# More groups in seven half products, a twelve-operation norm, and multiplies moved from GpSimd to VectorE in a fused attention and gated-MLP kernel

## The chip, the cores and the metric

The kernel runs on one core of a Trainium2 chip. Its engines are named as in the profile: PE is TensorE's matrix unit (PEld its weight loads), DVE is VectorE, ACT is ScalarE, POOL is GpSimd, and SP is SyncE, which here only starts transfers. The metric is the device time of one execution in microseconds (us), as the median of several runs.

## The reference

Inputs are q, k and v, each 8 batches × 8 heads × 576 rows × 64, a gain `g_norm` of 64, and four weight matrices: `w_gate` and `w_val` (512×1536), `w_out` (1536×512) and `w_res` (512×512). Everything is float32 in and out. Cut to what matters:

```python
kv  = einsum('bhsd,bhse->bhde', k, v)
o   = einsum('bhsd,bhde->bhse', q, kv)
o   = o / sqrt(mean(o*o, axis=-1) + 1e-6) * g_norm      # per head
x   = o.transpose(0, 2, 1, 3).reshape(4608, 512)
ffn = (gelu(x @ w_gate) * (x @ w_val)) @ w_out
out = x + sigmoid(x @ w_res) * ffn
```

So a linear attention without softmax, with a root-mean-square norm over each head, gives x. A gated MLP follows, and a sigmoid gate weighs its result before x is added back.

## The kernel before

**Blocks.** A batch gives 576 rows: 512 of them form one block, and the 64 left over of all eight batches together form a ninth block. Blocks 0 to 7 belong to batches 0 to 7; block 8 holds the remainders. While the MLP of block m runs on PE, the attention of batch m + 2 is prepared beside it.

**Slots.** The order of all instructions is written out by hand. Each block has sixteen slots. Slots 0 to 11 are the gate and value products of the twelve hidden slices f of 128; slots 12 to 15 are the two halves of the `w_res` product, then the out projection. Work of other engines is attached to a slot with `at(blk, slot, ...)`, to a point within the out projection with `aside_out`, and to a word within a group of products with `at_word`. An engine executes what it is given in that order, each instruction waiting for what it needs.

**A direct slice** (`m_gval`, L386) is four PE matmuls of 128×512 for the gate and four for the value; ACT applies GELU to the gate (L374) and DVE multiplies it with the value (L375) into `hid`.

**A group in half products** (`gv_group`) does four slices at once. Gate and value are each a 2×2 block product, done with seven half-size products in place of eight, in the manner of Strassen and Winograd. A product is four matmuls of 128×256. This needs four sums of quadrants of x (`token_sums`, once per block, in `ts`) and four of the weights (`weight_sums`, once per group and matrix, in `ws`), which DVE forms in fp16. The order of a group is one line of words (L762):

```python
"1g 1v Eg 5g Ev 5v dg 6g dv 6v Fg 2g Fv 2v 7g g11 7v cg 3g cv 3v h11 g22 4g g12 h12 4v g21 h22 h21"
```

A digit is a product of gate or value. E and d are copies on ACT, F and c additions on DVE that read PSUM, g11 to g22 the GELUs and h11 to h21 the hidden products, of which h22 runs on POOL and the others on DVE. The PSUM tiles are called A, E, F: products 1, 4, 6 and 7 go to A, 2 to E (which starts as a copy of A), 3 and 5 to F.

`GROUPS` (L1151) says which fours of slices are done so: groups 1 and 2 (f 4 to 11) in blocks 2 to 6, all three in blocks 7 and 8. Blocks 0 and 1 have only direct slices. `banks_of` assigns the eight PSUM banks: four serve the MLP (`pmoe`), four the attention (`pattn`), and a block with groups uses banks of both.

**The out projection** (`out_by_products`, L479) is done in seven half products too, with sums over `hid` in `hid_s` (`s_begin`, `s_rest`, `s_last`) and over `w_out` (`wo_sums`). Its results pass PSUM tiles w A, D, E, F; DVE multiplies them with the sigmoid gate into `osb` (L518), POOL adds x (`fin`, L522), and SP stores. In block 0 the projection goes slice by slice instead (`out_by_f`). In block 1 the fins were placed in the first four slots of block 2.

**Attention of a batch.** POOL issues seven loads (`load_batch`), behind a tiny copy `hold` that waits for an earlier transfer (`load_behind`). ACT squares the attention output and DVE reduces it per head (L254). `a_norm` forms the reciprocal root from these sums by a bit-level first guess and three steps; on POOL it takes fifteen operations (L300 to L312). `a_t` (L332, DVE) scales the attention output from PSUM into t; the PSUM bank is free when it has read it. `a_x` (L346) multiplies a row of t by g, and SP transposes the result into xT (`d_xT`). t times g is x itself, which `fin` adds at the end; for blocks 0 and 1 xT is made from t on PE and ACT (`a_xT`), so `a_x` is needed there only before the fins.

## Time and profile before

| | |
|---|---|
| median of 7 runs | 329.94 us (328.15 to 331.95) |
| profiled execution, own time | 330.35 us |
| its span | 328.5 us |
| mean granted PE clock | 0.995 |
| starts of block 1, 2, 3 on PE | 55.69, 92.93, 128.34 us |
| starts of block 4, 5, 6 | 161.88, 195.42, 229.22 us |
| starts of block 7, 8 | 260.98, 291.94 us |

The span is the time from the first to the last instruction of the profiled execution; its own time is 1.85 us longer. In timeline lines the columns are: start in us, duration in us, engine, line, operation, what is written and read (buffer names), and how many instructions follow each other without a gap (the duration is of all of them). In brackets stands the idle time before and what ended it. A line of waits reads: the waiting engine, buffer and line, what it waited for, the total in us, the count and the longest.

### The profile page before, as it was taken

What the parts mean: (1) busy time and instruction counts of PE and PEld (TensorE: products, weight loads), DVE (VectorE), ACT (ScalarE), POOL (GpSimd) and SP (SyncE); (2) the same over time, 40 slices, a digit from 0 to 9 for tenths busy, and PEclk for the clock granted to TensorE, in tenths of its full rate; (3) what the DMA queues carried; (4) which work ended last, traced back from release to release, by engine and by line L of the source; (5) the groups of instructions that cost most, each with busy time, mean ns of one, the idle gap of its engine ahead of it and who ended that gap; (6) DMA issues with size and microseconds to landing.
All of it is one profiled execution on the core that took longest, in us unless ns stands there. A gap on an engine that the chain in (4) does not pass through costs nothing.

```text
span 328.5 us, 7155 instructions
## 1 busy us (share of the span) xinstructions
PE 318.1 (97%) x2816; PEld 224.6 (68%) x2816; DVE 259.3 (79%) x463; ACT 191.2 (58%) x347; POOL 147.8 (45%) x225
## 2 busy tenths in 40 slices
PE   8899999999988999999999999999999999999993
PEld 3544455444846867686768686868587888788882
DVE  6757769679699788888887888697889877687754
ACT  3773485366626683768376846674465466636660
POOL 3792141573794378328731974115511331051232
PEclk9999999999999999999999999999999999999998
DMA  7999999699993689487937693800340030011004
GB/s 248 322 195 204 194 204 173 163 190 124 162 133 96 164 109 116 162 128 91 138 144 145 74 152 130 161 2 3 129 82 0 6 124 2 0 67 66 0 3 128
DMA packets 76692, 38.87 MB, mean 118 GB/s; under 512 B 42098, under 2 KB 74354, under 8 KB 76658
## 3 DMA queue, kind: packets, MB, share of 16 engines
q0 software_dynamic: 38752, 17.17, 41.9%
q1 hardware_dynamic: 37328, 20.71, 24.2%
q10 hardware_dynamic: 578, 0.52, 0.5%
q8 instruction: 22, 0.36, 0.4%
q14 instruction: 12, 0.10, 0.1%
HBM read 38.80 MB, written 9.44 MB: 147 GB/s over the span
## 4 chain that ended last, share of the span: by engine, by line
PE 89%; DVE 5%; DMA 2%; issue 1%; SPq 1%; ACT 1%; POOL 0%; DVEq 0%; ACTq 0%
PE wA L479 11%; PE gps L386 10%; PE vps L386 10%; PE rps L406 10%; PE Av L723 8%; PE Ag L723 8%; PE Fv L723 4%; PE Fg L723 4%; PE fps L423 3%; PE wD L479 3%; PE wE L479 3%; PE w L479 2%; PE wF L479 2%; PE Ev L723 2%; PE Eg L723 2%; DMA kf<-in_k_dram 2%
## 5 line engine op out<-in xcount | busy, mean ns | idle before, releaser
L374 ACT ACTIVATE ge<-gps 128x512 f16<-128x512 f32 x44 | 26.1, 597 | 56.1 <-PE gps L386 56.0
L760 POOL TENSOR_TENSOR hid<-ge,c 128x512 f16<-128x512 f16 x16 | 18.6, 1162 | 82.0 <-ACT ge L754 82.0
L723 PEld LDWEIGHTS <-ws 128*128 128x128 f16 x512 | 50.0, 98 | 7.3 <-issue 1.4
L386 PE MATMUL vps<-xT,wv 128*128 128x512 f16 x168 | 43.1, 379 | 0.3 <-DVE osb L518 0.3
L386 PE MATMUL gps<-xT,wg 128*128 128x512 f16 x168 | 43.1, 379 | 0.0
L522 POOL TENSOR_TENSOR osb<-osb,t 128x512 f32<-128x512 f32 x28 | 32.6, 1190 | 22.1 <-DVE osb L518 21.9
L375 DVE TENSOR_TENSOR hid<-ge,vps 128x512 f16<-128x512 f16 x44 | 29.9, 683 | 14.6 <-PE vps L386 12.1
L479 PEld LDWEIGHTS <-hid_s 128*128 128x128 f16 x384 | 37.6, 98 | 4.3
L406 PE MATMUL rps<-wr,xT 128*128 128x512 f16 x144 | 33.4, 380 | 0.0
L479 PEld LDWEIGHTS <-hid 128*128 128x128 f16 x288 | 28.2, 98 | 5.8 <-issue 0.8
L386 PEld LDWEIGHTS <-wv 128*128 128x128 f16 x168 | 16.4, 98 | 20.4 <-issue 0.8
L386 PEld LDWEIGHTS <-wg 128*128 128x128 f16 x168 | 16.3, 98 | 18.2 <-issue 0.2
L415 ACT ACTIVATE th<-rps 128x512 f32<-128x512 f32 x36 | 21.1, 594 | 8.5 <-PE rps L406 8.5
L254 DVE TENSOR_REDUCE ss<-sq 128x8 f32<-128x512 f32 x32 | 20.1, 678 | 7.3 <-ACT sq L249 7.3
L406 PEld LDWEIGHTS <-xT 128*128 128x128 f16 x144 | 13.5, 98 | 14.4
L744 DVE TENSOR_TENSOR Fg<-Ag,d 128x512 f32<-128x512 f32 x16 | 11.2, 700 | 14.8 <-PE Ag L723 12.2
L723 PEld LDWEIGHTS <-wg 128*128 128x128 f16 x192 | 18.5, 98 | 3.3
L479 PE MATMUL wA<-wo_ts,hid_s 128*128 128x256 f16 x168 | 20.6, 273 | 0.0
L723 PEld LDWEIGHTS <-wv 128*128 128x128 f16 x192 | 18.8, 98 | 2.2
L723 PE MATMUL Av<-ts,ws 128*128 128x256 f16 x128 | 19.2, 272 | 1.1 <-ACT Ev L733 1.1
L420 ACT ACTIVATE th<-th 128x512 f32<-128x512 f32 x36 | 20.1, 641 | 0.0
L754 ACT ACTIVATE ge<-c 128x512 f16<-128x512 f32 x16 | 10.1, 630 | 15.7 <-DVE c L744 15.7
(186 smaller groups left out, 704.2 us busy)
## 6 DMA issues: line engine op xcount, KB each, us to landing
out_dram<-osb SPq DMA_DIRECT2D x14, 512.0 KB, 2.6
qraw<-in_q_dram POOLq DMA_DIRECT2D x7, 512.0 KB, 6.7
k<-in_k_dram POOLq DMA_DIRECT2D x7, 512.0 KB, 10.4
v<-in_v_dram POOLq DMA_DIRECT2D x7, 512.0 KB, 11.8
wg<-in_moe_w_gate_dram POOLq DMA_DIRECT2D x2, 512.0 KB, 8.3
wv<-in_moe_w_val_dram POOLq DMA_DIRECT2D x2, 512.0 KB, 8.8
wo<-in_moe_w_out_dram POOLq DMA_DIRECT2D x2, 512.0 KB, 13.6
out_dram<-osb SPq DMA_DIRECT2D x4, 256.0 KB, 4.3
```

What stands on the lines that cost most here:

```text
L254: nc.vector.tensor_reduce(out=out_, in_=sqs.pop((b, i)), op=ALU.add, axis=mybir.AxisListType.X)
L374: nc.scalar.activation(out=ge, in_=gps, func=AF.Gelu)
L375: nc.vector.tensor_tensor(out=hids[blk][:, f, :], in0=ge, in1=vps, op=ALU.mult)
L386: nc.tensor.matmul(ps[:, j0 * P : j1 * P], lhsT=w[:, cc, :], rhs=xT_t[blk][:, j0:j1, cc, :], start=(cc == 0 and j0 == 0), stop=(cc == NP - ...
L406: nc.tensor.matmul(rps, lhsT=xT_t[blk][:, j, cc, :], rhs=wr16[:, cc, :], start=(cc == 0), stop=(cc == NP - 1),)
L415: nc.scalar.activation(out=th, in_=rps, func=AF.Tanh, scale=0.5)
L420: nc.scalar.activation(out=th, in_=th, func=AF.Copy, scale=0.5, bias=0.5)
L479: nc.tensor.matmul(ps[:, e - es[0], :], lhsT=a[:, f, e * P : (e + 1) * P], rhs=b[:, f, :], start=(start and e == es[0] and f == 0), stop=( ...
L522: nc.gpsimd.tensor_tensor(out=res_all[of], in0=res_all[of], in1=t_t[blk][of], op=ALU.add)
L723: nc.tensor.matmul(out_[:, r, :], lhsT=lhsT, rhs=rhs, start=(first and r == 0 and c == 0), stop=(c == 1), skip_group_check=True,)
L744: nc.vector.tensor_tensor(out=dst, in0=ps["A", u], in1=sb["d", u], op=ALU.add)
L760: eng.tensor_tensor(out=dst, in0=ge[q], in1=source(q, "v"), op=ALU.mult)
```

## The change

- **Block 0**: the last four slices (f 8 to 11) become a group of half products (`last_group`). The token sums of block 0 are formed on DVE ahead of its first hidden products. The weight sums of groups 1 and 2 are placed in other slots of block 0, and two of them at a word of the new group.
- **Block 6**: all three groups are in half products, in the order 0, 1, 2. With an odd number of groups the banks change roles. The later parts of batch 7's attention (`a_t`, `a_x` and the transposes) are placed at words of these groups. The weight sums of group 0, formed in block 6 before, are formed in the groups of blocks 2 to 5.
- **The norm on POOL** takes two steps with other constants: twelve operations in place of fifteen.
- **x of block 0** moves from slot 5 of block 0 to slot 15, still on DVE. **x of block 1** moves from POOL (block 2, slots 0 and 1) to DVE, at words of block 2's groups, and the fins and stores of block 1 move with it.
- **Memory**: some tiles share buffers now (`qr`, `qrT`, `wd`, small constants, the `o32` of batch 7), and the sums of group 0's weights have tiles of their own.

```diff
@@ tiles
-            qr_t[b // 2] = qkvp.tile([P, C], FP16, tag="qr", name="qr")
+            qr_t[b // 2] = qkvp.tile([P, C], FP16, tag="qr", bufs=1, name="qr")
-        st[b]["qrT"] = attnp.tile([P, NP, P], FP16, tag="qrT", name="qrT")
+        st[b]["qrT"] = attnp.tile([P, NP, P], FP16, tag="qrT", bufs=1, name="qrT")
-            w["d"] = finp.tile([P, 2, CH], FP32, tag="wd", bufs=1, name="wd")
+            w["d"] = attnp.tile([P, 2, CH], FP32, tag="o32", name="wd")
-                pool, tag = (wpool, f"ws{n}{g}") if g > 0 else (qkvp, "k16")
-                gv_sums[unit] = pool.tile([P, 4, 2, 2, P], FP16, tag=tag, name="ws")
+                gv_sums[unit] = wpool.tile([P, 4, 2, 2, P], FP16, name=f"ws{n}{g}")
@@ a_norm
+        magic = 0x5F1FFFF9 if eng is nc.gpsimd else 0x5F3759DF
+        if eng is nc.gpsimd:
+            for step in range(2):
+                eng.tensor_tensor(out=a, in0=yy, in1=yy, op=ALU.mult)
+                eng.tensor_tensor(out=a, in0=a, in1=m, op=ALU.mult)
+                c = (-0.703952253, 0.703952253 * 2.38924456) if step == 0 else (0.375, -1.25)
+                eng.tensor_scalar(out=mh, in0=a, scalar1=c[0], scalar2=c[1], op0=ALU.mult, op1=ALU.add)
+                if step == 1:
+                    eng.tensor_tensor(out=mh, in0=mh, in1=a, op=ALU.mult)
+                    eng.tensor_scalar(out=mh, in0=mh, scalar1=1.875, scalar2=None, op0=ALU.add)
+                eng.tensor_tensor(out=yy, in0=mh, in1=yy, op=ALU.mult)
+            return
@@ out_by_products
-            at(blk + 1, 0, lambda: fin((0, 0)))
-            at(blk + 1, 1, lambda: fin((0, 1)), lambda: store(0))
-            at(blk + 1, 2, lambda: fin((1, 0)))
-            at(blk + 1, 3, lambda: fin((1, 1)), lambda: store(1))
+            x = [lambda j=j: a_x(blk, j) for j in range(NJ)]
+            at_word(blk + 1, 0, "h21", *x[0:2], lambda: fin((0, 0)), lambda: fin((0, 1)), lambda: store(0))
+            at_word(blk + 1, 1, "Fv", x[2])
+            at_word(blk + 1, 1, "h21", x[3], lambda: fin((1, 0)), lambda: fin((1, 1)), lambda: store(1))
@@ attn_plan_1 (slot 15 of block 0)
+                *[lambda j=j: a_x(0, j) for j in range(NJ)],
-        return plan, [lambda j=j: a_x(b, j, nc.gpsimd) for j in range(NJ)]
+        return plan
@@ groups
-    GROUPS = {blk: (1, 2) for blk in range(2, B - 1)} | {B - 1: (1, 0, 2), B: (0, 1, 2)}
+    GROUPS = {blk: (1, 2) for blk in range(2, B - 2)} | {B - 2: (0, 1, 2), B - 1: (1, 0, 2), B: (0, 1, 2)}
@@ plan_attn_ahead
+        if b == B - 1:
+            t = [lambda j=j: a_t(b, j) for j in range(NJ + 1)]
+            x = [lambda j=j: a_x(b, j) for j in range(NJ + 1)]
+            for i, word, fs in (
+                (0, "1v", t[2:3]),
+                (0, "Fv", t[3:4]),
+                (0, "h21", t[4:5]),
+                (1, "1v", x[0:2]),
+                (1, "Fv", x[2:3]),
+                (2, "1v", [x[3], lambda: d_xT(b, 0, NJ), x[4], lambda: d_xT(b, NJ, NJ + 1)]),
+            ):
+                at_word(m + 1, i, word, *fs)
+            return
@@ weight sums
-    for slot, u in ((6, ("g", 1)), (8, ("v", 1)), (11, ("g", 2)), (13, ("v", 2))):
+    for slot, u in ((2, ("g", 1)), (4, ("g", 2)), (NF - 1, ("v", 1))):
+    at(0, 6, *sums["v", 2][0:2])
+    at_word(0, 0, "Fv", *sums["v", 2][2:4])
-    for i, f in enumerate(late_sums[0:4]):
-        at_word(B - 2, i // 2, ("Fv", "h21")[i % 2], f)
-    at(B - 2, NF + 1, *late_sums[4:8])
+    for i, f in enumerate(late_sums):
+        at_word(2 + i // 2, i % 2, "Fv", f)
@@ banks_of
+            if len(groups) % 2:
+                ga0, ga1, va0, va1, ge_, gf, ve, vf = ga1, ga0, va1, va0, gf, ge_, vf, ve
@@ main loop
-            slots = [first_gval, None]
+            slots = [lambda: first_gval(token_sums(0, nc.vector)), None]
-            slots += [lambda f=f: m_gval(0, f) for f in range(3, NF)]
+            slots += [lambda f=f: m_gval(0, f) for f in range(3, 2 * GF)]
+            def last_group():
+                x, t = pmoe.turn, pattn.turn
+                ends = {}
+                for i, u in enumerate("gv"):
+                    ends.update({(u, "A"): x[i], (u, "E"): x[2 + i], (u, "F"): t[i]})
+                pmoe.turn = x[2:] + x[:2]
+                pattn.turn = t[2:] + t[:2]
+                gv_group(0, 2, ends, amid_gv.get((0, 0), {}))
+            slots += [last_group, None, None, None]
-            plan[5] = [lambda j=j: a_x(0, j) for j in range(NJ)]
-            if blk == 2:
-                plan.setdefault(0, [])[0:0] = rows[0:2]
-                plan.setdefault(1, []).extend(rows[2:4])
```

## The prediction

> **What bounds the kernel now.** I read the page's busy line first, then the chain of work that ended last by engine, then TensorE's waits.

> ```profile
> PE 318.1 (97%) x2816; PEld 224.6 (68%) x2816; DVE 259.3 (79%) x463; ACT 191.2 (58%) x347; POOL 147.8 (45%) x225
> PE 89%; DVE 5%; DMA 2%; issue 1%; SPq 1%; ACT 1%; POOL 0%; DVEq 0%; ACTq 0%
> PE Av L723 <- ACT Ev L733: 1.1, 1, 1.1
> PE wA L479 <- DVE osb L454: 0.7, 1, 0.7
> PE vps L386 <- DVE osb L518: 0.3, 1, 0.3
> ```

> TensorE is busy for 318.1 of 328.5 us and carries 89% of the last chain, so the time falls only by fewer matmul columns or by removing one of its few stalls. The last three lines (wait, total, count, longest) are nearly all of those after the opening, and all stand around the front of block 2. TensorE's timeline gives the price of four hidden slices in either form (block 3):

> ```profile
> 128.34 1.03 PE L386 MATMUL gps<-xT,wg 128*128 128x512 f16 x4
> ...
> 135.25 0.60 PE L723 MATMUL Ag<-xT,wg 128*128 128x256 f16 x4
> ...
> 141.36 0.60 PE L723 MATMUL Ag<-xT,wg 128*128 128x256 f16 x4
> ```

> From the first start to the second, four direct slices take 6.91 us; a group of products takes 141.36 − 135.25 = 6.11 us, 0.437 per product. **A converted group is worth 0.79 us** if nothing waits.

> In block 2 the direct slices take 7.44 (92.93 to 100.37), 0.53 too much, and the first group 7.45 (to 107.82), 1.34 too much. VectorE's and GpSimd's timelines say why:

> ```profile
> 92.42 1.35 DVE L454 TENSOR_TENSOR ts<-xT,ts 128x512 f16<-128x512 f16 x1
> 93.69 1.64 DVE L518 TENSOR_TENSOR osb<-th,osb 128x512 f32<-128x512 f32 x1
> 100.04 2.46 DVE L346 TENSOR_TENSOR t<-t,g 128x512 f16<-128x512 f16 x2
> 228.72 0.42 DVE L454 TENSOR_TENSOR ts<-xT,ts 128x512 f16<-128x512 f16 x1
> 229.06 0.76 DVE L518 TENSOR_TENSOR osb<-th,osb 128x512 f32<-128x512 f32 x1
> 229.74 0.67 DVE L518 TENSOR_TENSOR osb<-th,wA 128x512 f32<-128x512 f32 x1
> 230.36 1.29 DVE L332 TENSOR_TENSOR t<-op,ny 128x512 f16<-128x512 f32 x2
> ```

> ```profile
> 92.34 2.45 POOL L346 TENSOR_TENSOR t<-t,g 128x512 f16<-128x512 f16 x2
> 99.76 2.45 POOL L522 TENSOR_TENSOR osb<-osb,t 128x512 f32<-128x512 f32 x2
> 123.21 0.22 POOL L300 TENSOR_SCALAR nm<-ss 128x40 f32<-128x40 f32 x1 [1.70 <-DVE ss L254]
> 230.06 0.27 POOL L312 TENSOR_TENSOR ny<-na,ny 128x40 f32<-128x40 f32 x1
> 230.29 4.49 POOL L522 TENSOR_TENSOR osb<-osb,t 128x512 f32<-128x512 f32 x4
> ```

> The same sums cost 1.35 and 1.64 at block 2's front, beside GpSimd's two x multiplies, and 0.42 and 0.76 at block 6's, where GpSimd is at its small norm. A pair of x multiplies takes 2.46 beside two fins and 0.75 alone.

> [...] the PSUM-fed rows stay at 0.67 to 0.69 beside the same GpSimd work. [...] the trace has 6.91/32 = 0.216 and 6.11/56 = 0.109.

> **The change part by part**, in us of this profiled execution (span 328.5, own time 330.35; the 1.85 around the span I leave alone).

> *Block 0's last group*: −0.79. Its added VectorE work is four token sums (0.42 each) and rearranged weight sums (about 0.48 per pair of halves). All run in VectorE's gaps except one: the third v2 weight sum stands behind add Fv, whose end in a group is about 3.66 after the group's start; with 0.42 the sum ends at 4.08, while TensorE wants it for 7v at 3.93 and its weight load 0.1 earlier. The wait is about 0.26 (bounds 0 to 0.5, if the sum before it is late too). Net **−0.53**.

> *x of block 1 off GpSimd*: the last token sum falls 1.35 → 0.42, the last residual product 1.64 → 0.75, the x pair 2.46 → 0.75. That is 0.93 + 0.89 + 1.71 us of VectorE time just ahead of the waits for `osb` and for Ev (which waited for VectorE's hidden product of slice 3), so 0.53 + 1.34 = **−1.88** if nothing new comes. The four rows now cost VectorE 4 × 0.37 = 1.5 us behind h21 and Fv, where it waits for TensorE's next sum; if that cover were gone they would cost at most these 1.5. Block 0's four rows stay on VectorE and only move from slot 5 to slot 15, where its out projection asks VectorE for little and their readers, the fins of block 1's first slots, are far off: 0.

> *What block 2 gives back*. GpSimd's order was x, x, fins, h22, h22, hold, the seven loads, norm; it becomes h22, fin, fin, h22, fin, fin, hold, loads, norm. The fins (1.15 each) now run late: the second pair waits for the x row behind group 2's h21 and runs beside the out stage's `hid_s` sums (0.95 each, two SBUF inputs), on which the last subtraction into wF depends; two collisions of up to 0.9 against the slack there leave about **+0.6** (0 to 0.9). Queued behind the fins are hold and seven DMA issues (116.04 to 121.51 on GpSimd's timeline, 5.5 us), and behind these the norm of batch 4. Two fins and the start of the first set the issues some 4.4 to 6.1 later in the block; 1.70 of this is slack (the norm's wait above), and the shorter norm returns 1.07. So the norm ends 1.4 to 3 late. VectorE's a_t of batch 4 waits for it, and hidden products f0 to f3 of block 3 are queued behind a_t; TensorE has 1.05 to 1.3 of slack before it needs the bank or Ev. Stall about **+1.0** (0.35 to 1.6). The loads themselves, 4 to 6 us later, are used a block later and hidden.

> *Norm on GpSimd in twelve operations*, six norms: three operations of about 0.27 plus 0.08 between, so 1.07 less. In the block ends of 3 to 5 the norm is not on the path, since a_t stands behind VectorE's own work: at 230.36, the norm done at 230.33. Gain 0. But the fins follow the norm on GpSimd: the first moves from 230.29 to about 229, onto the last token sum (228.72) and residual product (229.06), which then cost 0.9 more each when hit. In front of direct slices slack takes most of it (0 to 0.8 each): **+0.2** for two boundaries.

> *Block 6 in three groups*: −0.79. In place of direct slices, which use only banks of the out stage, its first products come at once: 1g, 1v, then 5g writes the F bank that holds batch 7's attention output until a_t has read it, and 5v the next. From 229.22, TensorE wants 5g at 230.09 and 5v at 230.53; the two a_t, behind VectorE's `osb` products, end at 231.0 and 231.65. So 5v waits at least 1.1 where before nothing waited. If the earlier fin hits one residual product (+0.9), 2.0; if two, 2.9. I take one: net **+1.2** (+0.4 to +2.3). Queued behind 5g is the whole of the block. The other a_t and x of batch 7, at words of the groups, just fit: two groups give VectorE about as much gap as they fill. The sums of group 0's weights, moved from block 6 to groups of blocks 2 to 5 (0.48 per pair), sit behind Fv, where VectorE has time until c.

> *Shared tiles*: qr and qrT in one buffer, wd in o32, constants in the tag of the gelu outputs: each earlier user has finished before the new one starts in the old timeline; 0. If one binds, it is at most one landing of a transfer, under the range's top.

> Sum: −0.53 − 1.88 + 0.6 + 1.0 + 0.2 + 1.2 = **+0.6**, own time 330.95. The profiled execution stands 0.41 above the median of 329.94, so **330.5**, in effect no change.

> **The rivals.** *B, the stalls simply vanish.* Block 2 gives nothing back because the slack behind the out stage is larger than I count, and block 6 waits the bare 1.1: −0.53 − 1.88 + 0.4 = −2.0, median **327.9**. For it: the page's waits of TensorE are few, and GpSimd is 45% busy, so 5 us of delay may find cover. Against it: the a_t at 230.36 is in VectorE's own order.
> *C, slower: collisions at the front of block 6 and wherever a fin comes early.* Place: the fin that now begins with the token sum and residual product of a block's front. Price: two hits each, block 6's wait 2.9 (+2.1 net), 0.8 at each of two other boundaries, with 0.6 + 1.2 in block 2: −0.53 − 1.88 + 0.6 + 1.2 + 1.6 + 2.1 = +3.1, **333.0**. It decides once the norm ends before about 228.7 of the old clock; at 1.07 earlier it ends at 229.26, so it needs 0.5 more. For it: each operation left out also drops its gap, and of the old norm's fifteen some took 0.5 to 0.63.
> *D, products alone.* The stalls of block 2 only move behind other work, and conversion pays in full: −1.59, **328.35**. Against it: 5v's wait.

> **How the numbers follow.** My forecast has 0.45 (its own range 329.2 to 331.9), B 0.20, C 0.25, D 0.10. The range reaches from B's time to just above C's: **328.0 to 333.2**. A measurement of this kernel tells about 0.5%, 1.65 us, from no change. Faster: most of B and half of D, 0.20; slower: most of C and the top of mine, 0.33; the same: 0.47.

> **What would show it.** In TensorE's timeline after: block 0's group at 6.1 to 6.4, with any wait at the gate's or value's seventh product; block 2's front at 6.91 and 6.11, without its three waits; in block 6 a wait of F's products for the a_t of 1 to 3 us; a wait for VectorE in block 3's direct slices. In GpSimd's: loads in block 2 some 5 us nearer the norm, the first fin of blocks 4 to 6 over a residual product of 1.65 instead of 0.75. The forecast is wrong if block 6's 5g does not wait (then B), if block 3's front has no gap, or if a wait appears in block 1's new x rows.

## The result and the profile after

The changed kernel takes 333.61 us in the median (331.60 to 336.89), beside 329.86 for the kernel before (all of its runs by then). The ratio is 1.012, with a 95% interval from 1.0099 to 1.014: slower by 1.2%. Executions in the slower state that a few runs of either kernel show are left out of the ratio. The profiled execution took 334.86 us, with a span of 333.1.

The page of the changed kernel, busy line and chain by engine:

```profile
PE 320.2 (96%) x2864; PEld 230.1 (69%) x2864; DVE 267.7 (80%) x477; ACT 195.0 (59%) x355; POOL 137.5 (41%) x205
PE 83%; DVE 9%; DMA 4%; issue 2%; POOL 0%; ACT 0%; DVEq 0%; ACTq 0%
```

TensorE is busy for 2.1 us *more* than before, though the change takes 16 × 512 × 4 − 28 × 256 × 4 = 4096 columns from it (two groups, at 0.79 us each). Longer busy time for fewer columns points to a slower clock somewhere, though only in part: the ends of matmuls are modelled in this view (products that start 0.44 apart are given 0.60 each), so a short wait counts as busy, and blocks 3 to 5 show 1.3 us more busy time (102.22 for 100.88) at full clock. The chain went from 5% to 9% VectorE. TensorE's waits after the opening (wait, total, count, longest):

```profile
PE Fg L735 <- DVE t L345: 2.6, 1, 2.6
PE wA L492 <- DVE osb L467: 1.0, 1, 1.0
PE vps L399 <- DVE osb L531: 0.7, 2, 0.3
PE vps L399 <- DVE hid L388: 0.6, 1, 0.6
```

The first starts of each block on TensorE's timeline give the account by blocks (us):

| stretch | before | after | difference | predicted |
|---|---|---|---|---|
| opening and block 0 | 55.69 | 55.20 | −0.49 | −0.53 |
| block 1 | 37.24 | 37.56 | +0.32 | 0 |
| block 2 | 35.41 | 33.54 | −1.87 | −1.88, and +0.6 given back |
| block 3 | 33.54 | 34.63 | +1.09 | +1.0 |
| block 4 | 33.54 | 34.33 | +0.79 | +0.2 for this and the next |
| block 5 | 33.80 | 34.60 | +0.80 | |
| block 6 | 31.76 | 35.60 | +3.84 | +1.2 |
| block 7 to the end | 67.52 | 67.64 | +0.12 | 0 |
| sum | 328.5 | 333.1 | +4.6 | +0.6 |

Blocks 0, 2 and 3 came out as worked out, block 2 without the 0.6 that it was to give back; blocks 4, 5 and 6 hold the error. The first row agrees in part by luck: in the runs below that share this opening, block 0's group starts anywhere from 30.98 to 31.70. The group itself took 6.33 us, where four direct slices take 6.91, so it is worth 0.58. Block 6's front in the changed kernel, on VectorE's, GpSimd's and TensorE's timelines:

```profile
229.36 1.38 DVE L467 TENSOR_TENSOR ts<-xT,ts 128x512 f16<-128x512 f16 x1
230.66 1.64 DVE L531 TENSOR_TENSOR osb<-th,osb 128x512 f32<-128x512 f32 x1
232.22 0.67 DVE L531 TENSOR_TENSOR osb<-th,wA 128x512 f32<-128x512 f32 x1
232.82 1.87 DVE L345 TENSOR_TENSOR t<-op,ny 128x512 f16<-128x512 f32 x3
```

```profile
224.73 0.22 POOL L306 TENSOR_SCALAR nm<-ss 128x40 f32<-128x40 f32 x1 [7.81 <-DVE ss L254]
...
229.07 0.27 POOL L319 TENSOR_TENSOR ny<-nh,ny 128x40 f32<-128x40 f32 x1
229.30 2.45 POOL L535 TENSOR_TENSOR osb<-osb,t 128x512 f32<-128x512 f32 x2
```

```profile
230.30 0.60 PE L735 MATMUL Av<-xT,wv 128*128 128x256 f16 x4
233.55 0.60 PE L735 MATMUL Fg<-ts,wsg 128*128 128x256 f16 x4 [2.65 <-DVE t L345]
234.15 0.60 PE L735 MATMUL Fv<-ts,wsv 128*128 128x256 f16 x4
234.58 0.87 PE L735 MATMUL Ag<-ts,wsg 128*128 128x256 f16 x4
...
238.43 0.60 PE L735 MATMUL Av<-ts,wsv 128*128 128x256 f16 x4
```

The norm now takes from 224.73 to 229.34, 4.61 us in place of 6.24 (224.09 to 230.33). The fins begin at 229.30, just ahead of the last token sum, and that sum and the residual product behind it both stretch, from 0.42 and 0.76 to 1.38 and 1.64. The attention tiles come 1.84 late, and 5g, wanted at 230.30 + 0.44 = 230.74, starts at 233.55, 2.81 late (the 2.65 in the view counts from the modelled end of 1v). From 234.58 to 238.43 five products take 3.85 us in place of 2.18. The view by windows shows why; after each window's bounds and length come busy time and instructions of PE, PEld, DVE, ACT and POOL, then the granted clock:

```profile
231.36:234.78 3.42, 1.23 (x10) 0.95 (x10) 3.33 (x5) 1.16 (x2) 2.65 (x3) 1.00 0.38 153
234.78:238.19 3.41, 3.41 (x18) 2.36 (x17) 1.99 (x3) 1.18 (x2) 0.00 (x0) 0.50 0.38 154
```

TensorE's clock was at half for 3.41 us, beginning 1.2 us after it had resumed. So block 6 is −0.79 for the group, +2.81 at 5g, +0.16 at 5v and +1.67 for the half clock: +3.85, against 3.84 measured.

### The profile page after: what moved, and what is told of

Read it like the earlier page. It is cut to its first block, busy times and chain, and to the rows that moved or that the text cites. A ratio compares the mean times of both kernels' runs of the same rounds, so it can differ in the third digit from the quotient of the medians.

```text
span 333.1 us, 7261 instructions
## 1 busy us (share of the span) xinstructions
PE 320.2 (96%) x2864; PEld 230.1 (69%) x2864; DVE 267.7 (80%) x477; ACT 195.0 (59%) x355; POOL 137.5 (41%) x205
## 4 chain that ended last, share of the span: by engine, by line
PE 83%; DVE 9%; DMA 4%; issue 2%; POOL 0%; ACT 0%; DVEq 0%; ACTq 0%
PE Av L735 10%; PE Ag L735 9%; PE wA L492 9%; PE rps L419 8%; PE vps L399 7%; PE gps L399 7%; PE Fv L735 5%; PE Fg L735 5%; PE fps L436 3%; DMA xT<-t 3%; PE Ev L735 2%; PE Eg L735 2%; PE wF L492 2%; PE w L492 2%; PE wD L492 2%; PE wE L492 2%
## 5 line engine op out<-in xcount | busy, mean ns | idle before, releaser
L772 POOL TENSOR_TENSOR hid<-ge,c 128x512 f16<-128x512 f16 x18 | 20.9, 1163 | 96.0 <-ACT ge L766 90.8
L387 ACT ACTIVATE ge<-gps 128x512 f16<-128x512 f32 x36 | 21.3, 597 | 45.3 <-PE gps L399 45.2
L535 POOL TENSOR_TENSOR osb<-osb,t 128x512 f32<-128x512 f32 x28 | 34.2, 1240 | 26.8 <-DVE osb L531 23.7
L399 PE MATMUL vps<-xT,wv 128*128 128x512 f16 x136 | 34.9, 379 | 1.3 <-DVE osb L531 0.7
L399 PE MATMUL gps<-xT,wg 128*128 128x512 f16 x136 | 34.9, 379 | 0.0
L735 PEld LDWEIGHTS <-wsg 128*128 128x128 f16 x288 | 28.3, 99 | 6.3 <-issue 2.8
L735 PEld LDWEIGHTS <-wsv 128*128 128x128 f16 x288 | 28.2, 98 | 4.9 <-issue 0.9
L388 DVE TENSOR_TENSOR hid<-ge,vps 128x512 f16<-128x512 f16 x36 | 24.3, 681 | 8.0 <-PE vps L399 7.4
L254 DVE TENSOR_REDUCE ss<-sq 128x8 f32<-128x512 f32 x32 | 20.1, 677 | 4.6 <-ACT sq L249 4.6
L735 PE MATMUL Av<-ts,wsv 128*128 128x256 f16 x144 | 22.1, 276 | 0.1
L735 PE MATMUL Ag<-ts,wsg 128*128 128x256 f16 x144 | 22.1, 277 | 0.0
```

The lines of the kernel that those rows point to most:

```text
L254: nc.vector.tensor_reduce(out=out_, in_=sqs.pop((b, i)), op=ALU.add, axis=mybir.AxisListType.X)
L387: nc.scalar.activation(out=ge, in_=gps, func=AF.Gelu)
L388: nc.vector.tensor_tensor(out=hids[blk][:, f, :], in0=ge, in1=vps, op=ALU.mult)
L399: nc.tensor.matmul(ps[:, j0 * P : j1 * P], lhsT=w[:, cc, :], rhs=xT_t[blk][:, j0:j1, cc, :], start=(cc == 0 and j0 == 0), stop=(cc == NP - ...
L535: nc.gpsimd.tensor_tensor(out=res_all[of], in0=res_all[of], in1=t_t[blk][of], op=ALU.add)
L735: nc.tensor.matmul(out_[:, r, :], lhsT=lhsT, rhs=rhs, start=(first and r == 0 and c == 0), stop=(c == 1), skip_group_check=True,)
```

## The experiments

**Theory A**: the shorter norm lets the fins start on top of the token sum and the residual product at each block's end, and block 6's group makes TensorE feel all of it. **Its rivals**: the added sums and moved attention pieces fill VectorE; the half clock has another cause than the idle gap. A second theory, **B**, is about block 1's end: the wait there is the landing of the transposed x. TensorE's last product of that block waits for `c22`, a VectorE row that writes `osb`, and the first token sum of block 2, which needs the transposed x, stands ahead of `c22`.

### Fifteen operations in the changed kernel

```diff
-        if eng is nc.gpsimd: ...   # two steps, twelve operations
+        # three steps, fifteen operations, as in the kernel before
```

> The changed kernel with the norm on POOL back at fifteen operations, all else as changed. Theory A (the shorter norm lets the first fin of a block start 1 us earlier, onto the last token sum and the residual product): the two rows return from 1.38 and 1.64 us to 0.42 and 0.76 at the ends of blocks 3, 4 and 5; blocks 4 and 5 lose their 0.8 us each, block 6's wait for the attention tile falls from 2.65 to about 1 us (1.8 less), and if the half-clock stretch after that wait (1.67 us) comes from the wait's length, it goes too; block 3 gets 1.07 longer, since its a_t waits for the norm itself. Sum -2.3 to -4.0 us against the changed kernel. Rival (the waits at the fronts of blocks 4 to 6 come from the added sums and the moved attention pieces, not from the norm): no change at blocks 4 to 6, and +1 us in all.

Measured: 331.63 us, ratio 1.0058 (1.0028 to 1.0087) to the kernel before. Blocks 4, 5 and 6 take 33.54, 33.81 and 32.13: the first two are back to the size before, and 5g waits 0.85 with no clock loss behind it. Block 3 rises to 35.82, 1.19 above the changed kernel. VectorE at block 6's front:

```profile
229.58 0.42 DVE L460 TENSOR_TENSOR ts<-xT,ts 128x512 f16<-128x512 f16 x1
229.92 0.76 DVE L524 TENSOR_TENSOR osb<-th,osb 128x512 f32<-128x512 f32 x1
```

The rows are short again. The median fell by 2.0 us from the changed kernel's, a little less than the 2.3 to 4.0 expected. A norm with *more* operations made the kernel faster, so the rival with the sums and the moved pieces fails for blocks 4 and 5.

### The fins held back, the norm still short

```diff
-            if not later:
+            if not later and not held:
                 fin((0, 0))
@@ behind the last residual product, blocks 2 to 5
+                nc.gpsimd.tensor_copy(out=hold, in_=res_all[0:1, 2, CH : CH + 1])
+                fin((0, 0))
```

> The changed kernel with one tiny POOL copy ahead of the fins of blocks 2 to 5; it reads a value that the residual product pf11 writes, so no fin starts before that product is done. The norm keeps twelve operations. Theory A: the same cure as fifteen operations without their cost in block 3: blocks 4 and 5 lose 0.8 us each, block 6's wait falls by 1.8 us, and the half-clock stretch of 1.67 us goes if the wait's length causes it: -3.4 to -5.1 us against the changed kernel, the block 3 stall of 1.1 us unchanged. Rival (what delays VectorE's rows is not the fin beside them): no change, or slower, since the fins end later.

Measured: 329.90 us, ratio 0.9991 (0.9965 to 1.0018). Blocks 4, 5 and 6 take 33.54, 33.81 and 32.01, and block 3 keeps its stall (34.76). Nothing but the fins' start and the tiny copy ahead of them differs, so their place is the cause at the three fronts. Block 2 of this profile took 35.23 though, 1.69 too much, without a wait of its own; its windows show another half-clock stretch:

```profile
89.83:93.25 3.42, 1.30 (x12) 1.17 (x12) 3.30 (x8) 0.00 (x0) 0.00 (x0) 1.00 1.66 187
93.25:96.66 3.41, 3.41 (x10) 1.21 (x8) 2.31 (x4) 0.60 (x1) 0.00 (x0) 0.50 0.81 61
```

It follows a wait of 2.12 us at block 1's last product, which lies in the first of these two windows.

### Block 6 with direct slices

```diff
-GROUPS = {blk: (1, 2) for blk in range(2, B - 2)} | {B - 2: (0, 1, 2), B - 1: (1, 0, 2), ...}
+GROUPS = {blk: (1, 2) for blk in range(2, B - 1)} | {B - 1: (1, 0, 2), ...}
```

Batch 7's pieces go back to their slots with it.

> The changed kernel with block 6 back at four direct slices and two groups, batch 7's attention pieces in their slots as before; the sums of group 0's weights stay in blocks 2 to 5. Theory A: with direct slices nothing of block 6 needs the attention banks for 7 us, so only a collision stall of about 0.8 us is left, as in blocks 4 and 5: block 6 takes 31.76 + 0.8 = 32.6 us in place of 35.60, -3.0 us against the changed kernel, and TensorE's clock stays at its full value there. Rival (the group is worth its 0.79 us, and the loss in block 6 is from elsewhere): +0.8 us.

Measured: 331.98 us, ratio 1.0056 (1.0028 to 1.0085). Block 6 takes 32.55, as expected: the same two stretched rows, but direct slices hide all but 0.8. The clock stays full. The median fell by 1.6 and not 3.0. Why is not shown: the runs spread from 329.98 to 334.40 at like mean clocks, and the profiled execution, with 330.32, is among the quickest.

### Zeros in the gap

```diff
                 seed(word[1])
+                if (blk, g) == (B - 2, 0) and word[1] == "g":
+                    add_zeros(21)   # 21 matmuls with zero weights onto A
```

> The changed kernel with 21 matmuls of 128x128 (zero weights, added to the A tile, so that the sums don't change) in block 6 ahead of the product that waits for the attention tile; a tile of zeros is written for them at the end of block 5. They fill TensorE's gap. Theory A (the idle gap of 2.65 us makes the granted clock fall to half for 3.2 us afterwards): the products after the gap take 0.44 us each from the start, -1.7 us against the changed kernel, with the wait itself unchanged. Rival (the clock falls for another reason, as the transfers in that stretch): the products take 0.86 us as before, no change.

Measured: 332.80 us, ratio 1.0107 (1.0076 to 1.0139). TensorE's timeline:

```profile
230.01 2.45 PE L779 MATMUL Ag<-xT,busy 128*128 128x256 f16 x21 [0.22 <-ACT Eg L747]
232.44 0.60 PE L737 MATMUL Fg<-ts,wsg 128*128 128x256 f16 x4
233.04 0.60 PE L737 MATMUL Fv<-ts,wsv 128*128 128x256 f16 x4
233.47 0.60 PE L737 MATMUL Ag<-ts,wsg 128*128 128x256 f16 x4
```

The wait for the attention tile is as long as before, but the products behind it take 0.44 each. Block 6 is 33.93, exactly 1.67 below the changed kernel's. So it was the idle gap that took the clock, not the transfers of that stretch; the last section sets such gaps side by side. The median fell by only 0.8 us, with runs from 331.40 to 333.34; why not by more is not shown.

### The short norm alone, in the kernel before

```diff
-        # three steps, fifteen operations
+        if eng is nc.gpsimd: ...   # two steps, twelve operations
```

> The kernel before with the norm on POOL in twelve operations, nothing else changed. Theory A (a shorter norm makes the fins collide with the token sum and the residual product ahead of each front): +0.8 us at the fronts of blocks 4, 5 and 6, where direct slices follow, and at block 3 also if its norm ends early enough: +2.4 to +3.2 us against the kernel before. Rival (a shorter piece of work on POOL gains or is hidden): 0 to -1 us.

Measured: 333.86 us, ratio 1.0136 (1.0069 to 1.0204); few runs, and they fall into two pairs, near 332 and near 336. Blocks 3 to 6 take 34.34, 34.34, 34.60 and 32.55: four fronts, +0.80 each, the upper end of what was expected. The profiled execution, of the higher pair, also has a wait of 3.15 us at the end of block 1 and a half-clock stretch after it. Taken alone, the part that only removes operations loses 3.2 us at these four fronts.

### x of block 1 alone, in the kernel before

```diff
-            at(blk + 1, 0, lambda: fin((0, 0)))   # ... four slots
+            at_word(blk + 1, 0, "h21", *x[0:2], lambda: fin((0, 0)), lambda: fin((0, 1)), lambda: store(0))
+            at_word(blk + 1, 1, "Fv", x[2])
+            at_word(blk + 1, 1, "h21", x[3], lambda: fin((1, 0)), lambda: fin((1, 1)), lambda: store(1))
```

> The kernel before with x of block 1 on VectorE at words of block 2's groups, its fins and stores with it, as in the changed kernel; the norm keeps fifteen operations. Theory A (block 2 gets its 1.9 us back, but the late fins and loads push the norm of batch 4): block 2 -1.9 us, block 3 +2.3 us, as the changed kernel with fifteen operations showed there; together about +0.4 us against the kernel before. Rival (block 3's stall comes from the sums of group 0's weights, which blocks 2 to 5 took over and this kernel does not): block 3 unchanged, -1.9 us in all.

Measured: block 2 at 33.55 (−1.86) and block 3 at 35.50 (+1.96), together +0.1; the time is 331.34, ratio 1.0069 (1.0044 to 1.0094). The rival is out as the main cause: this kernel's block 3 has no added weight sums, and the stall is there. Fifteen operations in the changed kernel gave +2.28; whether the sums make up the 0.3 between is not tested. That the median lies 2.4 above, where the blocks say 0.1, stays open in part: its runs spread from 329.27 to 334.59, and the five longest have mean clocks of 0.990 to 0.992.

In the changed kernel's own trace the mechanism of block 3 reads so, on GpSimd and then VectorE:

```profile
115.07 3.64 POOL L535 TENSOR_TENSOR osb<-osb,t 128x512 f32<-128x512 f32 x2 [1.84 <-DVE t L359]
...
119.39 0.97 POOL L120 DMA_DIRECT2D qraw<-in_q_dram  x1 [0.32 <-issue]
...
129.14 0.27 POOL L319 TENSOR_TENSOR ny<-nh,ny 128x40 f32<-128x40 f32 x1
```

```profile
129.44 1.29 DVE L345 TENSOR_TENSOR t<-op,ny 128x512 f16<-128x512 f32 x2 [1.95 <-POOL ny L319]
```

Late fins, then the loads, then the norm, and VectorE idle for 1.95 us ahead of a_t.

### The token sums of block 2 moved back, in the kernel before

```diff
-        for key, f in zip(("00", "22", "01", "11"), t):
+        for key, f in zip(("11",) * 4 if blk == 2 else ("00", "22", "01", "11"), t):
```

> The kernel before with the four token sums of block 2 moved behind VectorE's c22 and the third residual product of block 1, so that these no longer stand behind the sums' wait for the transposed x. Theory B (the wait at block 1's last product, 0.7 us in the profile of the kernel before, 1.0 in the changed one and up to 2.2 in the runs of this study, is the landing of that transfer in front of c22): the wait vanishes, -0.8 us or more, and the spread of the runs gets smaller. Rival (c22 is late for its own operands): no change.

Measured: 332.27 us, ratio 1.008 (1.0049 to 1.0112), so slower, where a gain was expected. The wait at block 1's end did vanish (36.42 in place of 37.24), but a longer one came in block 2 (37.10 in place of 35.41). TensorE's timeline:

```profile
97.64 1.02 PE L386 MATMUL vps<-xT,wv 128*128 128x512 f16 x4 [3.34 <-DVE osb L518]
```

All four sums now stood beside GpSimd's x rows, three of them stretched to 1.26 to 1.37, and the residual products behind them came late. Theory B had the wait's cause right and forgot who else runs where the sums were put.

### Four repairs at once

The held fins; the token sums of block 2 behind c22; x and fins of block 1 all at the end of block 2's first group; in block 5 the two attention tiles ahead of the last token sum and of two residual products.

```diff
@@ with the held fins of above
-            at_word(blk + 1, 0, "h21", *x[0:2], lambda: fin((0, 0)), lambda: fin((0, 1)), lambda: store(0))
-            at_word(blk + 1, 1, "Fv", x[2])
-            at_word(blk + 1, 1, "h21", x[3], lambda: fin((1, 0)), lambda: fin((1, 1)), lambda: store(1))
+            at_word(blk + 1, 0, "h21", *x[2:4], *x[0:2], lambda: fin((0, 0)), lambda: fin((0, 1)), lambda: store(0))
+            at_word(blk + 1, 0, "h21", lambda: fin((1, 0)), lambda: fin((1, 1)), lambda: store(1))
-        at(m, NF + 3, lambda: new_block(b), lambda: a_t(b, 0), lambda: a_t(b, 1))
+        if b == B - 1:
+            aside_out(m, "11", lambda: new_block(b), lambda: a_t(b, 0), lambda: a_t(b, 1))
+        else:
+            at(m, NF + 3, lambda: new_block(b), lambda: a_t(b, 0), lambda: a_t(b, 1))
-            aside_out(blk - 1, key, f)
+            aside_out(blk - 1, "last" if (blk, key) == (B - 2, "11") else key, f)
-            pf((1, 1), c22)
-            pf((1, 0), w["A"])
+            if "last" in amid:
+                pf((1, 0), w["A"])
+                aside("last")
+                pf((1, 1), c22)
+            else:
+                pf((1, 1), c22)
+                pf((1, 0), w["A"])
```

> The changed kernel with four repairs: the tiny copy ahead of the fins of blocks 2 to 5; the token sums of block 2 behind c22; all four x rows and fins of block 1 at the end of block 2's first group, so that the loads and the norm of batch 4 are not late; and in block 5 the two attention tiles that block 6's group waits for ahead of the last token sum and of the two last residual products. Theory A, with the four sizes as the traces gave them: blocks 3, 4 and 5 at 33.54, 33.54 and 33.8 us, block 1 at 36.4, block 6 at 31.76 - 0.79 = 31.0: 4.0 to 4.5 us below the kernel before, a ratio of about 0.987. Rival (a group in block 6 and the removed stalls give their time back elsewhere): within 1.5 us of the kernel before.

Measured: **326.69 us, ratio 0.9922 (0.9895 to 0.9949)**, faster than both kernels, with runs between 326.31 and 327.41 only. The blocks from 1 to 6 take 36.42, 33.54, 33.55, 33.54, 33.80 and 31.56. With all fins of block 1 early, the stall of block 3 is gone. From block 1 on, the view of waits holds none of TensorE. Block 6's front on VectorE:

```profile
224.91 1.29 DVE L345 TENSOR_TENSOR t<-op,ny 128x512 f16<-128x512 f32 x2
226.12 0.68 DVE L532 TENSOR_TENSOR osb<-th,wA 128x512 f32<-128x512 f32 x1
226.71 0.41 DVE L467 TENSOR_TENSOR ts<-xT,ts 128x512 f16<-128x512 f16 x1
```

The tiles are done at 226.2, when TensorE wants 5g (226.27). The gain is 2.2 us against that set's median of the kernel before and not the 4.0 to 4.5 expected, for two reasons: the kernel before was at 328.91 there and not at the profiled 330.35, most likely because its wait at block 1's end is not in every execution; and block 6 is 0.6 above what three groups should take.

### What each piece is worth in the repaired kernel

> The kernel with the four repairs, and in block 6 the attention tiles and x rows of batch 7 each one word later (behind the F or c additions in place of ahead of them). In the run of the four repairs block 6 takes 31.56 us, 0.6 above what three groups should give, in gaps of 0.04 to 0.17 us at products 6, 7 and 4, where the F and c additions stand behind these pieces on VectorE. Theory A: most of the gaps go, block 6 at 31.0 to 31.2 us, -0.4 to -0.6 us against the kernel with four repairs, 326.2 us. Rival (VectorE is full in this block and the gaps only move): within 0.2 us of it.

```diff
-                (0, "1v", t[2:3]), (0, "Fv", t[3:4]), ... (1, "1v", x[0:2]), (1, "Fv", x[2:3]),
+                (0, "Fv", t[2:3]), (0, "cv", t[3:4]), ... (1, "Fv", x[0:1]), (1, "cv", x[1:3]),
```

Measured: 326.96 us, ratio 0.9912 (0.988 to 0.9944), block 6 at 31.77. The rival was right in the main: the gaps at product 7 of the first two groups go, and the third group gets gaps of 0.30 and 0.36 at 5v and 6v. VectorE is full there, busy for 12.13 of the block's first 12.4 us. The next three were timed on the same chip beside it.

> The kernel with the four repairs, block 6 with four direct slices and two groups, batch 7's pieces in their slots. Theory A (a group there is worth 0.79 less its gaps of 0.6): block 6 at 31.8 us in place of 31.56, +0.2 us. Rival (the group in itself gains nothing once the waits are gone): 0 or faster.

```diff
-GROUPS = {...} | {B - 2: (0, 1, 2), B - 1: (1, 0, 2), B: (0, 1, 2)}
+GROUPS = {...} | {B - 1: (1, 0, 2), B: (0, 1, 2)}
```

Measured: 327.39 us, ratio 0.9918 (0.9893 to 0.9944), block 6 at 32.31. Three groups are worth 0.75 us in block 6, more than the 0.2 expected, because this front has gaps of its own, at the sixth and seventh value products (0.47 and 0.10).

> The kernel with the four repairs, block 0 with twelve direct slices, without token sums of block 0; the weight sums that stood at a word of its group stand at slot 7. Theory A: block 0's group was worth 0.5 to 0.6 us in the trace of the changed kernel: +0.55 us. Rival (block 1's last product waits for a transfer whose landing doesn't move with block 0, so time gained in block 0 is lost there; it doesn't hold where the token sums stand behind c22): 0.

```diff
-            slots += [last_group, None, None, None]
-    at_word(0, 0, "Fv", *sums["v", 2][2:4])
+    at(0, 7, *sums["v", 2][2:4])
```

Measured: 327.59 us, ratio 0.9932 (0.9903 to 0.9961). From the first matmul of slice 8 to the `w_res` products block 0 takes 6.90 us (31.02 to 37.92), where the changed kernel's group took 6.33 (31.66 to 37.99): +0.57, as expected.

> The kernel with the four repairs and the norm on POOL at fifteen operations. Theory A (with the fins held, the shorter norm is worth its length only where VectorE waits for it: at block 6's front, where the attention tiles now stand early and the norm ended 0.1 us before them): block 6 +0.9 to +1.1 us, the other blocks unchanged, about +1.0 us. Rival (the shorter norm is worth nothing anywhere): 0.

```diff
-        if eng is nc.gpsimd: ...   # twelve operations
+        # fifteen operations
```

Measured: 327.46 us, ratio 0.9929 (0.9907 to 0.9951). Block 6 takes 32.63, +1.07, the others are unchanged. So the short norm is worth about a microsecond, at the one front that waits for it, once its early end harms nobody. The held fins and the early fins of block 1 were not taken out of the repaired kernel one by one. The medians of these three lie 0.4 to 0.6 above the 326.96 beside them; the blocks of the traces are the sharper measure.

## Why the prediction was wrong

**Right**: the value of a group, with its loss at the seventh value product (0.20 seen, 0.26 predicted); the stalls of block 2 (−1.87 for −1.88); block 3's stall and its chain of fins, loads, norm and a_t (+1.09 for +1.0), which the run of that part alone confirmed in kind (+1.96, with fifteen operations); that 5g in block 6 waits for a_t where before nothing waited. The price of a matmul held too: at full clock the changed kernel's trace has 3.46/16 = 0.216 us for 512 columns (126.30 to 129.76) and 4.81/44 = 0.109 for 256 (140.40 to 145.21).

**The step that failed** is "three operations of about 0.27 plus 0.08 between, so 1.07 less", with "at 1.07 earlier it ends at 229.26". The norm became 1.63 us shorter. The trace of before has these at the norm's tail, and the cheap ones were used as the price:

```profile
228.76 0.51 POOL L307 TENSOR_TENSOR na<-na,nh 128x40 f32<-128x40 f32 x1
229.35 0.63 POOL L311 TENSOR_SCALAR na<-na 128x40 f32<-128x40 f32 x1
```

They stand beside VectorE's token sum (228.72) and residual product (229.06), and the three other operations of this norm that took over 0.4 stand beside earlier token sums. The shorter norm is done at 229.34, just before the last of the token sums begins (229.36). Against the block's front the norm's end moved from 1.11 after to 0.52 before, which on the old clock is 229.34 − 0.64 = 228.70. That is the point the prediction named for its rival C ("before about 228.7"), from which the fin takes two rows and not one. The stalls of blocks 4 to 6 follow: two rows late by 0.96 + 0.88 = 1.84, of which direct slices hide 1.05. By this count one hit of 0.9 would have cost blocks 4 and 5 nothing, so "+0.2 for two boundaries" became +1.59. In block 6, with no slices to hide it, 5g was 2.81 late and 5v 2.97, where the prediction had 1.1 for 5v with no hit, 2.0 with one and 2.9 with two. So C was the right case, with the right price; its sum of +3.1 was short mainly by the clock.

**Not foreseen at all** was the half clock, 1.67 us in the profiled execution.

**Too dark** was the +0.6 for late fins in block 2: no wait of TensorE came, so the slack behind the out stage covers them. **Left out** was block 1's +0.32: the last product waits for c22, which stands behind the token sum and so behind the transfer of xT, and that landed only 0.38 earlier (89.20 for 89.58) while TensorE came 0.49 earlier. That is 0.11 of it; the other 0.2 is a pause of VectorE behind the first token sum for which the trace shows no wait.

## What to carry to other kernels

Before making a task on a helper engine shorter, look at what is queued behind it there and whom that will meet: a task can be holding a collision off, and then a release tied to the victim's end is better than luck. Price removed instructions by the rows that are removed, not by the cheapest of their kind. And a stall of TensorE can cost its clock on top of its length: behind the 2.65 us in block 6 it ran at half clock for 3.41 us, another 1.67 lost.

## What the runs showed of the hardware

| kernel, place | idle in all, us | most of it in one window, us | clock in the next window |
|---|---|---|---|
| held fins, end of block 1 | 2.12 | 2.12 | half |
| fifteen operations, end of block 1 | 2.19 | 1.74 | full |
| changed, block 6 | 2.65 | 2.19 | half |
| short norm alone, end of block 1 | 3.15 | 3.15 | half |
| token sums moved, block 2 | 3.34 | 1.67 | full |

Full clock followed the longest gap, which fell half on one window and half on the next, 1.67 us each:

```profile
92.56:95.97 3.41, 1.74 (x9) 0.69 (x7) 3.41 (x4) 1.19 (x2) 3.33 (x3) 1.00 1.35 95
95.97:99.39 3.42, 1.75 (x8) 0.78 (x8) 3.42 (x6) 0.00 (x0) 3.34 (x4) 1.00 0.39 158
```

The traces of the two kernels hold 187 such windows. In three of them TensorE is idle for 2.19 us or more (2.19 in block 6 of the changed kernel; 2.20 before and 2.73 after, from its last product on), and half clock follows each; in the other 184 it is idle for at most 0.95 us, and half clock follows none. With the table, half clock followed 2.12 us and more and full clock 1.74 us and less, as the traces show idle time, with the ends of matmuls modelled; nothing between the two is shown here. The steps lie elsewhere in each of the two profiled executions (from 7.85 and from 9.49 us), so a gap may fall on one window in one execution and on two in another; that this decides whether the clock is lost is an estimate. The runs with the moved token sums fit it: four with a mean clock of 0.999 took 330.66 to 331.82, the six others, with 0.994 or less, 332.26 to 333.43. The mean clock alone is no measure of the loss, though, since it also falls behind TensorE's last product: the profile of the kernel before has 0.995 without half clock amid the work. The clock makes 1.67 of the 4.6 us between the two profiled executions; how much of the 3.75 us between the medians it makes is not known.

**The landing of one transfer differed by 3.8 us between the traces.** The transposed x of batch 2 took 8.1 to 10.7 us from issue to landing beside the loads of batch 3 (9.09 in the kernel before, 9.29 in the changed one); a block later such a transfer took 4.4 in both. Landings from 87.7 to 91.5 us made the wait at block 1's end anything from none to 3.15 us. With the sums behind c22 and no x rows on GpSimd, the wait is gone, and the runs of the repaired kernel lie within 1.1 us. That the narrow spread comes from this repair and not from the other three is not shown.
